# Interleaving the first block products of a second MLP with the last products of the first, on one Trainium2 core

## The chip, the cores and the metric

The kernel runs on one core of one Trainium2 chip. The metric is device time in microseconds, the median of several executions. A core has five engines with queues of their own: TensorE (PE, the matrix engine, whose weight loads are listed apart as PEld), VectorE (DVE), ScalarE (ACT), GpSimd (POOL) and SyncE (SP), which here only issues transfers. They wait for each other through semaphores; each works its own queue strictly in order.

## What is computed

Three stages on 2304 tokens, all in fp32 (cut to what matters):

```python
attn = softmax(mask(q @ k.T / sqrt(D))) @ v          # 4 x 8 heads, window 32, half of them dilated by 4
x  = attn laid out as (2304, 512)
xn = x / rms(x) * rms_g
u  = silu(xn @ w_gate) * (xn @ w_val)                # 1536 hidden
x  = u @ w_out                                       # (2304, 512)
h  = x @ w_in                                        # (2304, 1024)
e  = exp(h - max(h)); solu = h * e / sum(e)
ln = (solu - mean) / sqrt(var + 1e-6) * g_ln
out = ln @ w_out2                                    # (2304, 512)
```

## The kernel before, in words

**Products.** Every fp32 operand is split into a rounded high part and a rest, and a product is three matmuls: high by high, high by low, low by high (`mm3`, lines 849 to 851; 1110 to 1112; 1182 to 1184). One matmul has 512 columns.

**The first MLP** (`mlp`, 853) goes over the tokens in seven stretches; the last five of 512 tokens (the very last part, p = 4, has 512). For each of 12 blocks f of the hidden size: `g` (12 matmuls, gate), `vp` (12, value), then on ACT and DVE tanh (L880), two products (L886, L890) and the split into `uh` (L286, L295), and two blocks later `out` (12 matmuls into four accumulators y0 to y3). After the last block the accumulators are copied to `yo` (L286/L290) and stored to memory as `yT`.

**The second MLP** goes over pairs of tiles of 128 tokens, r = 0 to 8, two tiles each. One pair:

- `p_load` (1052) reads the pair's activations `y` back from `yT` with three transfers (L1056, L1058).
- `p_sums` (L1064) makes four sums of blocks, on POOL or DVE; `p_high` and `p_low` (L286, L295) split them into `yh`, first three blocks (128x768), then four (128x1024).
- Seven block products `p1` to `p7` of six matmuls each (`p_product`, L1110 to L1112): a Strassen-Winograd scheme, into accumulators `ha` to `hd`. p1, p6 and p7 add up in `ha`, and after each of them `ha` is copied out (s1, u2, u3: L286 or L290) before the next may write. p5 and p3 share `hb`. Four sums on DVE (`p_sum`, L1118; named c11, c12, c21, c22 below) put the rows of h together: c22 needs u3 and p5, c21 p4, c12 p3, c11 p2.
- For each of the two tiles (row 1, then row 0): exp (ACT, L1128), solu (DVE, L1135), square (ACT, L1142), centre (DVE, L1147) and a root on POOL (L1151, L1152).

One tile then takes eight transposes `t` (L1163), the split into `lt` (L286 on ACT, then L295 on DVE: "lt low"), 24 matmuls `o` (L1182 to L1184) in two halves of 12, an evacuation `ob` and a store (L1200).

**Order.** A planner (`Plan.order`, 165) gives every step an engine and a place from estimated costs, due times and needs; the instructions are then issued in that order, and each engine works its queue in order. For TensorE the order of the second MLP is written out by hand (the list `line`, 1299): each step is put behind the one ahead of it.

```python
line = [("out", last, NF1 - 1, 1)] + h(0, "p1", "p5", "p6", "p2", "p7", "p4") + h(1, "p1") + h(0, "p3") + \
    h(1, "p2", "p5", "p6", "p7", "p4", "p3") + t(0)
```

So no product of a pair is issued ahead of the first MLP's last `out`. The room for odd pairs' `y` and `yh` (pool `hp`) is opened by `switch` (1207), which needs all steps of the first MLP; only pair 0 (and 2, once 0 is done) has room earlier, where the attention's was.

Of the kernel before, what the change touches and what calls it, by code (L numbers as in the profile page):

```python
# [240 lines left out]
def tile_attention_glu_solu(ctx: ExitStack, tc: tile.TileContext, qk_d, v_d, w1_d, win2_d, wout2_d,  # L241
# [68 lines left out]

    def prepare(stage, f, cuts, srcs, scales, dues, needs=(), lead=((1, 0), "joined", 0)):

# [4 lines left out]
        def raw(c):  # L317
            if ("raw", key, c) not in T:
                T["raw", key, c] = wp.tile([P, len(c), 512, 2], I32, tag=f"w{f}_{c[0]}", name=f"raw{f}_{c[0]}")
            return T["raw", key, c]  # L320
# [34 lines left out]
        def halves(c):  # L355

            def emit(e):
                T["th", key, c] = wp.tile([P, len(c), 2, 512], F32R, tag=f"w{f}_{c[0]}", name=f"w{f}_{c[0]}")
                put(e, T["th", key, c][:, :, 0], wf_(c))
            return emit  # L360

        def lows(c):
            def emit(e):
                th = T["th", key, c]
                less(e, th[:, :, 1], wf_(c), th[:, :, 0])
                for i in c:
                    (w1 if stage == 1 else w2)[f, i] = th[:, i - c[0]]
            return emit
# [699 lines left out]
    def p_high(r, h, e):  # L1068
        if r not in pairs:
            pairs[r] = pool["y", r % 2].tile([P, 2, 7, 2, P], F32R, tag=f"yh{r % 2}", name="yh")  # L1070
        c = SETS[h]
        put(e, pairs[r][:, 0, c], y2[r][:, 1 + c.start:1 + c.stop])

    def p_low(r, h, e):
        c = SETS[h]
        less(e, pairs[r][:, 1, c], y2[r][:, 1 + c.start:1 + c.stop], pairs[r][:, 0, c])

# [26 lines left out]
    def p_product(r, a, b, bank, more):  # L1104
        o, yh = p_bank(r, bank), pairs[r]
        for j in range(2):
            x = LEFT[a]
            w = w_in[b, j]
            first, last_ = j == 0 and not more, j == 1
            nc.tensor.matmul(o, yh[:, 0, x, j], w[:, 0], start=first, stop=False, skip_group_check=True)  # L1110
            nc.tensor.matmul(o, yh[:, 0, x, j], w[:, 1], start=False, stop=False, skip_group_check=True)
            nc.tensor.matmul(o, yh[:, 1, x, j], w[:, 0], start=False, stop=last_, skip_group_check=True)  # L1112

# [60 lines left out]
    def p_products(i, ks, a=0, n=DM):  # L1174
# [5 lines left out]
        for k in ks:  # L1180
            w = w2[5 + k // 3, k % 3][:, :, a:a + n]
# [21 lines left out]
    def second_stage(stage_1, last):  # L1203
# [3 lines left out]
        def switch(e):  # L1207
            p1.close()
            pool["hp"] = pool["y", 1] = ctx.enter_context(tc.tile_pool(name="hp", bufs=1))

        def opened(e):
            pa.close()
            pool["y", 0] = ctx.enter_context(tc.tile_pool(name="yp", bufs=1, side="right"))
            pool["sp2"] = ctx.enter_context(tc.tile_pool(name="sp2", bufs=2, side="right"))
# [4 lines left out]
        def pair_steps(r):  # L1219
            due = base + 22 * (r - 2)  # L1220
            ys, yh, hw, ew = ((x + str(r % 2), (x, r)) for x in ("ys", "yh", "hw", "ew"))
            p = max(x for x in range(len(PARTS)) if start[x] <= r * TP)
            add(("load", r), {"s": 1.6}, lambda e: p_load(r), [("opened",) if r % 2 == 0 else ("switch",)] +
                [("store", p, k) for k in range(KD)], takes=[ys], due=due - 40)
            add(("sums", r), {"p": 2.9, "d": 1.4}, lambda e: p_sums(r, e), [("load", r)], uses=[ys[1]], due=due - 20)
            for h, (a, d) in enumerate(((0.85, 0.95), (1.1, 1.25))):
                add(("yhigh", r, h), {"a": a}, lambda e, h=h: p_high(r, h, e), [("load", r)] + ([("sums", r), ("yhigh", r, 0)] if h else []),
                    takes=[yh] if h == 0 else [], uses=[ys[1], yh[1]], due=due - 20)
                add(("ylow", r, h), {"d": d}, lambda e, h=h: p_low(r, h, e), [("yhigh", r, h)], uses=[ys[1], yh[1]], due=due - 20)
            banks = {x: ("h" + x, r) for x in "abcd"}  # L1230
            tags = dict(a="g", b="vp", c="a", d="a")

# [4 lines left out]
            def kept(x, after_, tile_, tags_):  # L1237
                add((x, r), {"a": 0.6, "d": 0.62}, lambda e: put(e, p_row(r, x), p_bank(r, "a")), [(after_, r)],
                    takes=tags_, uses=[banks["a"], tile_[1]], due=due - 60)

            def total(x, row, col, kept_, bank, n, before):
                add((x, r), {"d": 0.75}, lambda e: p_sum(r, row, col, kept_, bank, n), before + [(kept_, r)],
                    uses=[banks[bank], hw[1], ew[1]], due=due - 50)

# [13 lines left out]
            total("c12", 0, 1, "u2", "b", 1, [("p3", r), ("c11", r)])  # L1258
            for row in (1, 0):
                k = (r, row)  # L1260
                ends = [("c21", r)] if row else [("c12", r)]
                add(("neg", *k), {"d": 0.16}, lambda e, row=row: p_neg(r, row), ends, due=due - 10)
                add(("exp", *k), {"a": 1.3}, lambda e, row=row: p_exp(r, row), [("neg", *k)], uses=[hw[1], ew[1]], due=due)
                add(("solu", *k), {"d": 1.85}, lambda e, row=row: p_solu(r, row), [("exp", *k)], uses=[hw[1], ew[1]], due=due)
# [4 lines left out]
        def tile_steps(i):  # L1269
            r, row = divmod(i, 2)  # L1270
            due = base + 22 * r + 11 * row
            lt = ("lt", ("lt", i))
            for q in range(2):
# [4 lines left out]
                add(("lt", i, q, 1), {"d": 0.7}, lambda e, q=q: p_lt(i, q, 1, e), [("lt", i, q, 0)], uses=[tp[1], lt[1]], due=due - 60)  # L1278
            for a, n in ([(0, DM)] if i < NT2 - 1 else [(0, DM // 2), (DM // 2, DM // 2)]):
                o = (f"y{2 + (i + (a > 0)) % 2}", ("o", i, a))  # L1280
# [25 lines left out]
        line += [("o", NT2 - 1, a, q) for a in (0, DM // 2) for q in range(2)]  # L1306
        for x, y in zip(line, line[1:]):
# [29 lines left out]
    for j in range(2):  # L1337
        operands(j, done)
    for f in range(5, 8):
        us = range(3 * (f - 5), min(3 * (f - 5) + 3, NF2))  # L1340
        prepare(2, f, [(i,) for i in range(len(us))] if f < SINGLE else [tuple(range(len(us)))],
                [wout2_d[u] for u in us], [gln[:, u:u + 1] for u in us], [5070 + u for u in us], done(f), (("in", 0), "joined", "b11"))

    second_stage([x for x in plan.steps if x[0] not in ("evac", "store")], last)
# [92 lines left out]
```

## Time and profile before

| | |
|---|---|
| Time, median of 3 runs | 752.02 us (751.43 to 752.91) |
| The profiled execution | 749.95 us, span 748.2 us |
| PE busy | 734.1 us, 98% of the span |
| DVE, ACT, POOL busy | 59%, 43%, 17% |
| Granted clock of TensorE, mean | 0.995 |
| First MLP's last matmul to first `o` matmul | 537.3 to 567.9 us |

A busy PE is not one at its peak: matmuls overlap, so the distance between the starts of two matmuls that follow each other is the measure, and where it is longer than usual something was waited for or the clock was low. The timeline gives starts; the list of waits says which engine ended a wait; the windows give the granted clock of a stretch, where 1.00 is 2.4 GHz and 0.5 is 1.2 GHz.

### The profile page before, as it was taken

What the parts mean: (1) busy time and instruction counts of PE and PEld (TensorE: products, weight loads), DVE (VectorE), ACT (ScalarE), POOL (GpSimd) and SP (SyncE); (2) the same over time, 40 slices, a digit from 0 to 9 for tenths busy, and PEclk for the clock granted to TensorE, in tenths of its full rate; (3) what the DMA queues carried; (4) which work ended last, traced back from release to release, by engine and by line L of the source; (5) the groups of instructions that cost most, each with busy time, mean ns of one, the idle gap of its engine ahead of it and who ended that gap; (6) DMA issues with size and microseconds to landing.
All of it is one profiled execution on the core that took longest, in us unless ns stands there. A gap on an engine that the chain in (4) does not pass through costs nothing.

```text
span 748.2 us, 11769 instructions
## 1 busy us (share of the span) xinstructions
PE 734.1 (98%) x4637; PEld 613.0 (82%) x4637; DVE 439.3 (59%) x868; ACT 322.4 (43%) x734; POOL 130.7 (17%) x156
## 2 busy tenths in 40 slices
PE   8899999999999999999999999999989999999997
PEld 6788888899988888888887888888858888888886
DVE  4879996455433354434454438978278677655552
ACT  2876645355323233223334224534255555434340
POOL 0320322222300022300121204310023211001110
PEclk9999999999999999999999999999999999999999
DMA  8997003142121121041212036231111210101001
GB/s 330 405 404 275 26 11 111 69 150 88 39 88 37 39 75 51 1 157 37 82 55 74 1 94 228 72 113 56 60 54 54 66 52 29 47 25 28 30 29 42
DMA packets 34247, 68.91 MB, mean 92 GB/s; under 512 B 3344, under 2 KB 13584, under 8 KB 34192
## 3 DMA queue, kind: packets, MB, share of 16 engines
q1 hardware_dynamic: 34192, 68.16, 26.0%
q8 instruction: 36, 0.59, 0.3%
q14 instruction: 19, 0.16, 0.1%
HBM read 58.71 MB, written 9.44 MB: 91 GB/s over the span
## 4 chain that ended last, share of the span: by engine, by line
PE 94%; DMA 3%; DVE 1%; ACT 1%; SPq 0%; issue 0%; DVEq 0%
PE y L849 7%; PE g L849 7%; PE vp L849 7%; PE g L850 7%; PE g L851 7%; PE y L851 7%; PE y L850 7%; PE vp L851 7%; PE vp L850 7%; PE o L1183 4%; PE o L1184 4%; PE o L1182 4%; PE pv L631 2%; PE tp L1163 2%; PE sp L585 2%; PE ha L1112 2%
## 5 line engine op out<-in xcount | busy, mean ns | idle before, releaser
L849 PE MATMUL y<-uh,w 128*128 128x512 f32 (+1 forms) x244 | 91.6, 376 | 0.0
L851 PE MATMUL y<-uh,w 128*128 128x512 f32 (+1 forms) x244 | 89.2, 366 | 0.0
L850 PE MATMUL y<-uh,w 128*128 128x512 f32 (+1 forms) x244 | 89.1, 365 | 0.0
L886 DVE SCALAR_TENSOR_TENSOR u<-u,g 128x512 f32<-128x512 f32 (+1 forms) x61 | 38.1, 624 | 79.0 <-ACT u L880 78.6
L880 ACT ACTIVATE u<-g 128x512 f32<-128x512 f32 (+1 forms) x61 | 33.4, 547 | 118.4 <-PE g L851 118.4
L849 PE MATMUL vp<-xh,w 128*128 128x512 f32 (+1 forms) x196 | 77.9, 397 | 0.0
L849 PE MATMUL g<-xh,w 128*128 128x512 f32 (+1 forms) x196 | 77.6, 396 | 0.0
L850 PE MATMUL g<-xl,w 128*128 128x512 f32 (+1 forms) x196 | 75.9, 387 | 0.0
L851 PE MATMUL g<-xh,w 128*128 128x512 f32 (+1 forms) x196 | 75.9, 387 | 0.0
L851 PE MATMUL vp<-xh,w 128*128 128x512 f32 (+1 forms) x196 | 75.7, 386 | 0.0
L850 PE MATMUL vp<-xl,w 128*128 128x512 f32 (+1 forms) x196 | 75.5, 385 | 0.0
L890 DVE SCALAR_TENSOR_TENSOR u<-u,vp 128x512 f32<-128x512 f32 (+1 forms) x61 | 38.1, 625 | 49.9 <-PE vp L851 49.4
L286 ACT CAST uh<-u 128x512 fp32r<-128x512 f32 (+1 forms) x61 | 34.8, 570 | 74.0 <-DVE u L890 73.6
L1182 PE MATMUL o<-w,lt 128*128 128x512 f32 (+1 forms) x152 | 58.9, 388 | 0.0
L1184 PE MATMUL o<-w,lt 128*128 128x512 f32 (+1 forms) x152 | 57.6, 379 | 0.0
L1183 PE MATMUL o<-w,lt 128*128 128x512 f32 (+1 forms) x152 | 57.5, 379 | 0.0
L731 POOL TENSOR_TENSOR sq<-x 128x256 f32<-128x256 f32 x28 | 18.6, 666 | 211.6 <-DVE x L290 179.5
L295 DVE TENSOR_TENSOR uh<-u,uh 128x512 fp32r<-128x512 f32 (+1 forms) x61 | 43.8, 717 | 15.1 <-ACT uh L286 14.5
L849 PEld LDWEIGHTS y<-uh,w 128*128 128x128 f32 x244 | 46.0, 188 | 8.1
L851 PEld LDWEIGHTS y<-uh,w 128*128 128x128 f32 x244 | 46.0, 188 | 7.5
L850 PEld LDWEIGHTS y<-uh,w 128*128 128x128 f32 x244 | 46.1, 189 | 7.0
L598 ACT ACTIVATE s<-s,nm 128x64 f32<-128x64 f32 x120 | 40.2, 338 | 22.7 <-DVE nm L593 22.7
(165 smaller groups left out, 1580.5 us busy)
## 6 DMA issues: line engine op xcount, KB each, us to landing
raw<-w SPq DMA_DIRECT2D x36, 512.0 KB, 10.2
vt<-v SPq DMA_DIRECT2D x30, 256.0 KB, 2.7
qk<-qk SPq DMA_DIRECT2D x14, 400.0 KB, 3.5
yT<-yo SPq DMA_DIRECT2D x16, 256.0 KB, 2.5
raw<-win SPq DMA_DIRECT2D x8, 512.0 KB, 6.2
raw<-wout SPq DMA_DIRECT2D x8, 512.0 KB, 3.6
out<-ob SPq DMA_DIRECT2D x16, 256.0 KB, 2.0
qk<-qk SPq DMA_DIRECT2D x6, 448.0 KB, 4.2
```

Source lines behind the costliest of these rows:

```text
L286: nc.scalar.copy(dst, src) if scale is None else nc.scalar.mul(dst, src, scale)
L295: ENG[e].tensor_tensor(dst, a, b, ALU.subtract)
L598: nc.scalar.activation(T[s_][:, i], T[s_][:, i], AF.Exp, bias=st["nm"][:, i:i + 1], accum_out=sm[:, i:i + 1])
L849: nc.tensor.matmul(acc, wh, xh, start=first, stop=False)
L850: nc.tensor.matmul(acc, wh, xl, start=False, stop=False)
L851: nc.tensor.matmul(acc, wl, xh, start=False, stop=last)
L880: return lambda e: nc.scalar.activation(new(up, ("u", v, f), [P, 512])[:, 0:n], T["g", v, f], AF.Tanh, scale=0.5)
L886: return lambda e: nc.vector.scalar_tensor_tensor(out=u_of(f), in0=u_of(f), scalar=1.0, in1=T["g", v, f], op0=ALU.add, op1=ALU.mult)
L890: return lambda e: nc.vector.scalar_tensor_tensor(out=u_of(f), in0=u_of(f), scalar=0.5, in1=T["vp", v, f], op0=ALU.mult, op1=ALU.mult)
L1182: nc.tensor.matmul(o, lt[:, 0, k], w[:, 0], start=(k == 0), stop=False)
L1183: nc.tensor.matmul(o, lt[:, 0, k], w[:, 1], start=False, stop=False)
L1184: nc.tensor.matmul(o, lt[:, 1, k], w[:, 0], start=False, stop=(k == NF2 - 1))
```

## The change

The products of pair 0 are put between the products of the first MLP's last four blocks; pair 1's activations are loaded once the last but two `out` is issued, into the room of weight block 9, and its split parts go into room beside weight block 7 and into a tile of their own; pair 0's four accumulators use the two banks of tag `a` that the attention had; its c12 is summed ahead of its c11. In every pair the second tile goes ahead of the first through `t` and `o`. The weights of the last product move between blocks (one from block 7 to block 2). Pieces of the diff:

```diff
     def p_load(r):
-        y = pool["y", r % 2].tile([P, 8, 2, P], F32, tag=f"y{r % 2}", name="y")
+        if r == 0:
+            y = pool["yp"].tile([P, 8, 2, P], F32, tag="yl", name="y")
+        elif r == 1:
+            y = wp.tile([P, 8, 2, P], F32, tag="w9_0", name="y")
+        else:
+            y = pool["hp"].tile([P, 8, 2, P], F32, tag=f"y{r % 2}", name="y")
...
         if r not in pairs:
-            pairs[r] = pool["y", r % 2].tile([P, 2, 7, 2, P], F32R, tag=f"yh{r % 2}", name="yh")
+            if r % 2 == 0:
+                t = pool["yp"].tile([P, 2, 7, 2, P], F32R, tag="yh", name="yh")
+                pairs[r] = t[:, 0], t[:, 1]
+            else:
+                t = T["th", (2, 7), (0,)][:, 1:3].rearrange("p i h n -> p (i h n)")[:, 0:7 * TP]
+                pairs[r] = (t.rearrange("p (x j q) -> p x j q", x=7, j=2),
+                            pool["yp"].tile([P, 8, 2, P], F32R, tag="yl", name="yl")[:, 0:7])
...
+    SEQ = [i ^ 1 for i in range(NT2)]
+    OUT_AT = [(2, 2)] + [(f, i) for f in (5, 6) for i in range(3)] + [(7, 0)]
...
-            add(("load", r), {"s": 1.6}, lambda e: p_load(r), [("opened",) if r % 2 == 0 else ("switch",)] +
-                [("store", p, k) for k in range(KD)], takes=[ys], due=due - 40)
+            add(("load", r), {"s": 1.6}, lambda e: p_load(r), [("opened",) if r < 2 else ("switch",)] +
+                ([("out", last, 9, 1)] if r == 1 else []) + [("store", p, k) for k in range(KD)], takes=[ys],
+                due=due - 90 if r else 4900)
...
-            tags = dict(a="g", b="vp", c="a", d="a")
+            tags = dict(a="g", b="vp", c="a", d="a") if r else dict(a="a", b="a", c="a", d="a")
...
-            due = base + 22 * r + 11 * row
+            due = base + 22 * r + 11 * (1 - row)
...
-        line = [("out", last, NF1 - 1, 1)] + h(0, "p1", "p5", "p6", "p2", "p7", "p4") + h(1, "p1") + h(0, "p3") + \
-            h(1, "p2", "p5", "p6", "p7", "p4", "p3") + t(0)
+        def m(x, f):
+            return [(x, last, NF1 + f, i) for i in range(2)]
+
+        line = m("out", -4) + h(0, "p1") + m("g", -2) + h(0, "p5") + m("vp", -2) + h(0, "p6") + m("out", -3) + m("g", -1) + \
+            h(0, "p7") + m("vp", -1) + h(0, "p3") + m("out", -2) + h(0, "p2", "p4") + m("out", -1) + \
+            h(1, "p1", "p5", "p6", "p2", "p7") + t(SEQ[0]) + h(1, "p4", "p3")
         for q in range(NP):
-            a, b, r = 2 * q, 2 * q + 1, q + 2
-            line += h(r, "p1", "p5", "p6") + [("o", a, 0, 0)] + t(b) + [("o", a, 0, 1)] + h(r, "p2", "p7", "p4")
+            (a, b), r = SEQ[2 * q:2 * q + 2], q + 2
+            line += h(r, "p1", "p5", "p6") * (q > 0) + [("o", a, 0, 0)] + t(b) + [("o", a, 0, 1)] + \
+                h(r, "p1", "p5", "p6") * (q == 0) + h(r, "p2", "p7", "p4")
             if q < NP - 1:
-                line += [("o", b, 0, 0)] + h(r, "p3") + t(b + 1) + [("o", b, 0, 1)]
+                line += [("o", b, 0, 0)] + h(r, "p3") + t(SEQ[2 * q + 2]) + [("o", b, 0, 1)]
```

In the changed kernel the lines from 1056 on have moved: a product of a pair is at L1125 to L1127, a sum at L1133, the transposes at L1180, `o` at L1199 to L1201.

On TensorE, in the first MLP's last stretch, the change has this behind the fourth last `out` (y3 its last accumulator; win are the second MLP's weights, yh pair 0's split activations):

```order
L851 MATMUL y3_4572<-uh_5030,w8_0_1157 128x512
L1125 MATMUL ha_5109<-win_4633,yh_4577 128x512
L1126 MATMUL ha_5109<-win_4633,yh_4577 128x512
L1127 MATMUL ha_5109<-win_4633,yh_4577 128x512
L1125 MATMUL ha_5109<-win_4740,yh_4577 128x512
L1126 MATMUL ha_5109<-win_4740,yh_4577 128x512
```

This is p1 of pair 0. p5, p6, p7, p3, p2 and p4 follow in the same way between the `g`, `vp` and `out` that come after, where before all of them stood behind the last `out`.

On the SP queue, at the end of the first MLP, the loads of the pairs (y from yT, three transfers a pair) and the stores of the last results (yT from yo) stand so in the change:

```order
L324 DMA raw_0_5051<-wout 128x1024
L1061 DMA y<-yT_91 128x4x128
L1063 DMA y<-yT_91 128x2x128 x2
L957 DMA yT_95<-yo 128x512 x2
L1061 DMA y<-yT_92 128x4x128
```

Before, pair 1's load (from yT_91) stood behind all four of these stores. Now it stands ahead of them, and waits for the last matmul that reads weight block 9.

On VectorE, behind pair 0's centring (e) come pair 1's sums (h from hc, hb, hd, and hb again: c11, c22, c21, c12) and the first tile's lt low:

```order
L1162 TENSOR_SCALAR e<-e,st 128x1024 x2
L1133 ISA h,st<-h,hc 128x512
L1133 ISA st 128x1
L1133 ISA h,st<-e,hb 128x512
L1133 ISA st 128x1
L1133 ISA h,st<-e,hd,st 128x512
L1133 ISA st 128x1
L1133 ISA h,st<-h,hb,st 128x512
L1133 ISA st 128x1
L295 TENSOR_TENSOR lt<-tp,lt 128x512 x2
```

All four sums of pair 1 stand ahead of the first lt low. On TensorE the first `o` matmuls stand right behind p3 of pair 1, the product that the fourth of these sums reads; before, the eight transposes of a tile and three products of pair 2 stood between.

## Rows read from the trace of the kernel before

**Rows 1.** The page, part 1: busy us (share of the span) x instructions of each engine

```profile
PE 734.1 (98%) x4637; PEld 613.0 (82%) x4637; DVE 439.3 (59%) x868; ACT 322.4 (43%) x734; POOL 130.7 (17%) x156
```

**Rows 2.** TensorE's waits, whole span: us in total, times, longest us

```profile
PE ha L1112 <- DVE st L1133: 2.4, 1, 2.4
...
PE ha L1110 <- ACT h L286: 0.7, 1, 0.7
PE ha L1110 <- ACT yh L286: 0.3, 1, 0.3
```

**Rows 3.** Timeline of TensorE, 537 to 568 us: start, length (us), line, tiles, [idle <-releaser]

```profile
537.31 0.39 PE L1110 MATMUL ha<-win,yh 128*128 128x512 f32 x1
...
545.25 0.39 PE L1112 MATMUL hd<-win,yh 128*128 128x512 f32 x1
545.97 0.50 PE L1110 MATMUL ha<-win,yh 128*128 128x512 f32 x1 [0.33 <-ACT yh L286]
546.30 0.40 PE L1111 MATMUL ha<-win,yh 128*128 128x512 f32 x1
549.14 0.65 PE L1112 MATMUL ha<-win,yh 128*128 128x512 f32 x1 [2.45 <-DVE st L1133]
...
552.89 0.39 PE L1112 MATMUL hb<-win,yh 128*128 128x512 f32 x1
...
557.00 0.39 PE L1112 MATMUL ha<-win,yh 128*128 128x512 f32 x1
558.06 0.50 PE L1110 MATMUL ha<-win,yh 128*128 128x512 f32 x1 [0.68 <-ACT h L286]
...
562.80 1.09 PE L1163 MATMUL tp<-ident,e 128*128 128x128 f32 x8
563.65 0.47 PE L1110 MATMUL ha<-win,yh 128*128 128x512 f32 x1
...
567.86 0.39 PE L1182 MATMUL o<-w,lt 128*128 128x512 f32 x1
```

**Rows 4.** Busy us by stretch: length, PE, PEld, DVE, ACT, POOL, granted clock, DMA share, GB/s

```profile
34.00:45.00 11.00, 8.62 (x73) 8.10 (x73) 7.45 (x17) 7.95 (x16) 2.57 (x2) 1.00 1.03 409
545.60:549.10 3.50, 0.77 (x3) 0.30 (x2) 3.29 (x11) 2.40 (x4) 0.00 (x0) 1.00 0.01 2
549.10:553.00 3.90, 3.85 (x10) 3.05 (x11) 2.79 (x6) 1.92 (x4) 0.08 (x1) 0.56 0.00 0
```

**Rows 5.** Timeline of ScalarE, 545 to 564 us (columns as in rows 3)

```profile
545.08 0.83 ACT L286 CAST yh<-y 128x768 fp32r<-128x768 f32 x1 [0.18 <-DMA y<-yT]
...
557.42 0.58 ACT L286 COPY h<-ha 128x512 f32<-128x512 f32 x1 [0.57 <-PE ha L1112]
...
562.84 1.15 ACT L1128 ACTIVATE e<-h,st 128x1024 f32<-128x1024 f32 x1 [2.54 <-DVE st L1124]
```

**Rows 6.** Timeline of VectorE, 548 to 574 us

```profile
548.14 0.95 DVE L295 TENSOR_TENSOR yh<-y,yh 128x768 fp32r<-128x768 f32 x1
...
553.33 0.75 DVE L1118 CUSTOM_DVE_ANT_0 h<-h,hb,st 128x512 f32<-128x512 f32 x1 [1.33 <-PE hb L1112]
...
564.92 1.28 DVE L295 TENSOR_TENSOR lt<-tp,lt 128x512 fp32r<-128x512 f32 x2
...
566.49 1.28 DVE L1135 SCALAR_TENSOR_TENSOR e<-e,st,h 128x1024 f32<-128x1024 f32 x1
...
573.46 0.76 DVE L1147 TENSOR_SCALAR e<-e,st 128x1024 f32<-128x1024 f32 x1 [0.34 <-ACT sq L1142]
```

**Rows 7.** Timeline of GpSimd, 556 us

```profile
556.83 3.95 POOL L1064 TENSOR_TENSOR y<-y 128x256 f32<-128x256 f32 x4 [3.08 <-DMA y<-yT]
```

**Rows 8.** Timeline of the SP queue, 540 us

```profile
540.75 0.54 SPq L1056 DMA_DIRECT2D y<-yT  x1
```

**Rows 9.** Timeline of the SP queue, the end of the span

```profile
744.65 1.11 SPq L1200 DMA_DIRECT2D out<-ob  x2
```

**Rows 10.** Line L1200, the output stores: from issue to landing

```profile
DMA to landing us min/median/max: 1.9/2.0/2.6
```

More of the change, by code (lines that the diff above doesn't have):

```diff
@@ L309, in tile_attention_glu_solu, with prepare @@
     w1, w2 = {}, {}
-    def prepare(stage, f, cuts, srcs, scales, dues, needs=(), lead=((1, 0), "joined", 0)):
+    def prepare(stage, f, cuts, srcs, scales, dues, needs=(), lead=((1, 0), "joined", 0), at_=0, spare=0):
         key = (stage, f)
@@ L318, in raw @@
             if ("raw", key, c) not in T:
-                T["raw", key, c] = wp.tile([P, len(c), 512, 2], I32, tag=f"w{f}_{c[0]}", name=f"raw{f}_{c[0]}")
+                T["raw", key, c] = wp.tile([P, len(c), 512, 2], I32, tag=f"w{f}_{at_ + c[0]}", name=f"raw{f}_{c[0]}")
             return T["raw", key, c]
@@ L357, in emit @@
             def emit(e):
-                T["th", key, c] = wp.tile([P, len(c), 2, 512], F32R, tag=f"w{f}_{c[0]}", name=f"w{f}_{c[0]}")
-                put(e, T["th", key, c][:, :, 0], wf_(c))
+                T["th", key, c] = wp.tile([P, len(c) + spare, 2, 512], F32R, tag=f"w{f}_{at_ + c[0]}", name=f"w{f}_{c[0]}")
+                put(e, T["th", key, c][:, 0:len(c), 0], wf_(c))
             return emit
@@ L364, in emit @@
                 th = T["th", key, c]
-                less(e, th[:, :, 1], wf_(c), th[:, :, 0])
+                less(e, th[:, 0:len(c), 1], wf_(c), th[:, 0:len(c), 0])
                 for i in c:
-                    (w1 if stage == 1 else w2)[f, i] = th[:, i - c[0]]
+                    (w1 if stage == 1 else w2)[f, at_ + i] = th[:, i - c[0]]
             return emit
@@ L1069, in p_high @@
         if r not in pairs:
-            pairs[r] = pool["y", r % 2].tile([P, 2, 7, 2, P], F32R, tag=f"yh{r % 2}", name="yh")
+            if r % 2 == 0:
[5 more added lines that the diff above has]
+                            pool["yp"].tile([P, 8, 2, P], F32R, tag="yl", name="yl")[:, 0:7])
         c = SETS[h]
-        put(e, pairs[r][:, 0, c], y2[r][:, 1 + c.start:1 + c.stop])
+        put(e, pairs[r][0][:, c], y2[r][:, 1 + c.start:1 + c.stop])
     def p_low(r, h, e):
         c = SETS[h]
-        less(e, pairs[r][:, 1, c], y2[r][:, 1 + c.start:1 + c.stop], pairs[r][:, 0, c])
+        less(e, pairs[r][1][:, c], y2[r][:, 1 + c.start:1 + c.stop], pairs[r][0][:, c])
     LEFT = {"a11": 0, "a12": 1, "a22": 2, "s1": 3, "s2": 4, "s3": 5, "s4": 6}
@@ L1087, in p_row @@
     def p_row(r, x):
+        if x == "u3" and r == 0:
+            if (r, x) not in keep:
+                keep[r, x] = pool["yp"].tile([P, 512], F32, tag="u3", name="u3")
+            return keep[r, x]
         if x in ("s1", "u2") or x[0] == "h":
@@ L1109, in p_product @@
             first, last_ = j == 0 and not more, j == 1
-            nc.tensor.matmul(o, yh[:, 0, x, j], w[:, 0], start=first, stop=False, skip_group_check=True)
-            nc.tensor.matmul(o, yh[:, 0, x, j], w[:, 1], start=False, stop=False, skip_group_check=True)
-            nc.tensor.matmul(o, yh[:, 1, x, j], w[:, 0], start=False, stop=last_, skip_group_check=True)
+            nc.tensor.matmul(o, yh[0][:, x, j], w[:, 0], start=first, stop=False, skip_group_check=True)
+            nc.tensor.matmul(o, yh[0][:, x, j], w[:, 1], start=False, stop=False, skip_group_check=True)
+            nc.tensor.matmul(o, yh[1][:, x, j], w[:, 0], start=False, stop=last_, skip_group_check=True)
     def p_sum(r, row, col, kept, bank, n):
@@ L1208, in switch @@
             p1.close()
-            pool["hp"] = pool["y", 1] = ctx.enter_context(tc.tile_pool(name="hp", bufs=1))
+            pool["hp"] = ctx.enter_context(tc.tile_pool(name="hp", bufs=1))
         def opened(e):
             pa.close()
-            pool["y", 0] = ctx.enter_context(tc.tile_pool(name="yp", bufs=1, side="right"))
+            pool["yp"] = ctx.enter_context(tc.tile_pool(name="yp", bufs=1, side="right"))
             pool["sp2"] = ctx.enter_context(tc.tile_pool(name="sp2", bufs=2, side="right"))
@@ L1222, in pair_steps @@
             p = max(x for x in range(len(PARTS)) if start[x] <= r * TP)
-            add(("load", r), {"s": 1.6}, lambda e: p_load(r), [("opened",) if r % 2 == 0 else ("switch",)] +
-                [("store", p, k) for k in range(KD)], takes=[ys], due=due - 40)
-            add(("sums", r), {"p": 2.9, "d": 1.4}, lambda e: p_sums(r, e), [("load", r)], uses=[ys[1]], due=due - 20)
+            if r < 2:
+                ys = (("yh1", hw[0])[r], ys[1])
+            add(("load", r), {"s": 1.6}, lambda e: p_load(r), [("opened",) if r < 2 else ("switch",)] +
+                ([("out", last, 9, 1)] if r == 1 else []) + [("store", p, k) for k in range(KD)], takes=[ys],
+                due=due - 90 if r else 4900)
+            add(("sums", r), {"p": 2.9, "d": 1.4}, lambda e: p_sums(r, e), [("load", r)], uses=[ys[1]], due=due - 55 if r else 4900)
             for h, (a, d) in enumerate(((0.85, 0.95), (1.1, 1.25))):
-                add(("yhigh", r, h), {"a": a}, lambda e, h=h: p_high(r, h, e), [("load", r)] + ([("sums", r), ("yhigh", r, 0)] if h else []),
-                    takes=[yh] if h == 0 else [], uses=[ys[1], yh[1]], due=due - 20)
-                add(("ylow", r, h), {"d": d}, lambda e, h=h: p_low(r, h, e), [("yhigh", r, h)], uses=[ys[1], yh[1]], due=due - 20)
+                add(("yhigh", r, h), {"a": a}, lambda e, h=h: p_high(r, h, e), [("load", r)] + ([("sums", r), ("yhigh", r, 0)] + ([("uhigh", last, NF1 - 1)] if r == 1 else []) if h else [((2, 7), "halves", 0)] * (r % 2)),
+                    takes=[yh] if h == 0 else [], uses=[ys[1], yh[1]], due=due - 55 if r else 4900)
+                add(("ylow", r, h), {"d": d}, lambda e, h=h: p_low(r, h, e), [("yhigh", r, h)] + ([("ulow", last, NF1 - 1)] if (r, h) == (1, 1) else []), uses=[ys[1], yh[1]], due=due - 55 if r else 4900)
             banks = {x: ("h" + x, r) for x in "abcd"}
-            tags = dict(a="g", b="vp", c="a", d="a")
+            tags = dict(a="g", b="vp", c="a", d="a") if r else dict(a="a", b="a", c="a", d="a")
             def product(x, a, b, bank, more, before):
@@ L1238, in kept @@
                 add((x, r), {"a": 0.6, "d": 0.62}, lambda e: put(e, p_row(r, x), p_bank(r, "a")), [(after_, r)],
-                    takes=tags_, uses=[banks["a"], tile_[1]], due=due - 60)
+                    takes=tags_, uses=[banks["a"], tile_[1]], due=due - 60 if r else 4900)
             def total(x, row, col, kept_, bank, n, before):
                 add((x, r), {"d": 0.75}, lambda e: p_sum(r, row, col, kept_, bank, n), before + [(kept_, r)],
-                    uses=[banks[bank], hw[1], ew[1]], due=due - 50)
+                    uses=[banks[bank], hw[1], ew[1]], due=due - 50 if r else 4900)
             product("p1", "a11", "b11", "a", False, [])
@@ L1250, in pair_steps @@
             product("p2", "a12", "b21", "c", False, [])
-            total("c11", 0, 0, "s1", "c", 0, [("p2", r)])
+            total("c11", 0, 0, "s1", "c", int(r == 0), [("p2", r)] + [("c12", 0)] * (r == 0))
             product("p7", "s3", "t3", "a", True, [("u2", r)])
-            kept("u3", "p7", ew, [ew])
+            kept("u3", "p7", ew, [ew] if r else [])
             total("c22", 1, 1, "u3", "b", 0, [("p5", r)])
@@ L1257, in pair_steps @@
             product("p3", "s4", "b22", "b", True, [("c22", r)])
-            total("c12", 0, 1, "u2", "b", 1, [("p3", r), ("c11", r)])
+            total("c12", 0, 1, "u2", "b", int(r > 0), [("p3", r)] + [("c11", r)] * (r > 0))
             for row in (1, 0):
+                due = (due if r else 4950) + 1 + (row == 0)
                 k = (r, row)
-                ends = [("c21", r)] if row else [("c12", r)]
+                ends = [("c21", r)] if row else [("c12" if r else "c11", r)]
                 add(("neg", *k), {"d": 0.16}, lambda e, row=row: p_neg(r, row), ends, due=due - 10)
-                add(("exp", *k), {"a": 1.3}, lambda e, row=row: p_exp(r, row), [("neg", *k)], uses=[hw[1], ew[1]], due=due)
+                add(("exp", *k), {"a": 1.3}, lambda e, row=row: p_exp(r, row), [("neg", *k)] + ([("exp", 0, 1)] if k == (0, 0) else []),
+                    takes=[ew] if k == (0, 1) else [], uses=[hw[1], ew[1]], due=due)
                 add(("solu", *k), {"d": 1.85}, lambda e, row=row: p_solu(r, row), [("exp", *k)], uses=[hw[1], ew[1]], due=due)
@@ L1278, in tile_steps @@
                 add(("lt", i, q, 1), {"d": 0.7}, lambda e, q=q: p_lt(i, q, 1, e), [("lt", i, q, 0)], uses=[tp[1], lt[1]], due=due - 60)
-            for a, n in ([(0, DM)] if i < NT2 - 1 else [(0, DM // 2), (DM // 2, DM // 2)]):
+            for a, n in ([(0, DM)] if i != SEQ[-1] else [(0, DM // 2), (DM // 2, DM // 2)]):
                 o = (f"y{2 + (i + (a > 0)) % 2}", ("o", i, a))
@@ L1338, in tile_attention_glu_solu @@
         operands(j, done)
[L1339 to L1342, printed above, removed]
+    for f, us in ((2, (0,)), (5, (1, 2, 3)), (6, (4, 5, 6)), (7, (7,))):
+        prepare(2, f, [(i,) for i in range(len(us))], [wout2_d[u] for u in us], [gln[:, u:u + 1] for u in us],
+                [5070 + u for u in us], done(f), (("in", 0), "joined", "b11"), 2 if f == 2 else 0, 2 if f == 7 else 0)
     second_stage([x for x in plan.steps if x[0] not in ("evac", "store")], last)
```

4 lines of the change are left out of this document (2 added, 2 removed).

## The prediction

> **What bounds the kernel now.** I read the busy times first: TensorE is busy for 98% of the span [rows 1], so time can be gained only where it waits, runs at the low clock, or after its last matmul. Next, the list of TensorE's waits: the longest of the second half, 2.4 us, stands in front of `ha`, and two more of 0.7 and 0.3 us as well [rows 2]. The timeline then shows where they lie [rows 3]. From the first `ha` matmul at 537.31 to a matmul of `hd` at 545.25 there are 35 steps (from start to start) in 7.94 us, 0.227 us a step; this is the pace of unhindered matmuls of 512 columns. From 537.31 to the first `o` matmul at 567.86, 30.55 us, TensorE issues 102 such matmuls (14 products of pairs 0 and 1, three of pair 2, six matmuls each) and one set of transposes, 0.85 us long (562.80 to 563.65). 102 x 0.227 + 0.85 = 24.0 us. So 6.55 us are lost here. After this stretch a pair repeats at full pace, and the list of waits holds nothing for it.
>
> **What the lost time is made of** [rows 3].
> a) 545.25 to 549.14: three steps take 3.89 us in place of 0.68, so 3.21 lost. Pair 1's activations are late: their load is issued at 540.75 [rows 8], behind the whole first MLP, and is ready for ScalarE's cast at 545.08 [rows 5], 4.3 us later; sums and the low part follow, the latter until 549.09 [rows 6].
> b) 549.14 to 552.89: nine steps take 3.75 us in place of 2.04, so 1.71 lost. The granted clock of 549.10 to 553.00 is 0.56, that is for most of it the lower of the two levels (1.2 GHz in place of 2.4), after a stretch in which TensorE was busy for 0.77 of 3.50 us [rows 4].
> c) 557.00 to 558.06: one step of 1.06, so 0.83 lost; p7 of pair 1 stands right behind p6 and waits until `ha` is copied out.
> d) The remaining 0.80 are small: longer first steps after each wait, a short wait in front of p3, and the edges of the transposes.
>
> **What the change does to each.**
> Pair 0's seven products move in between the first MLP's matmuls. The matmuls stay the same in number, so this by itself gives nothing. It gives cover: once the last `out` is issued, pair 1's operands have long been there. Their load now waits for the third last `out` only. Behind that come g, p7, vp, p3, out, p2, p4 and out: 72 matmuls, 16.3 us. The path is 4.3 us to the cast, four sums on GpSimd 3.95 [rows 7], the cast of the four-block part (4/3 of 0.83, 1.1) and its low part (4/3 of 0.95, 1.3): 10.7 us. It fits with 5 us to spare, so a) goes, and with it b). c) goes because p2 now stands between p6 and p7 of pair 1: 1.36 us of matmuls over a copy of 0.58 [rows 5]. Of d) I take 0.5. Gained: 3.21 + 1.71 + 0.83 + 0.5 = 6.25 us; the bounds are 5.75 (nothing of d) and 6.55.
>
> The work that pair 0 hands to other engines must be hidden in the first MLP:
> - s1 (p1 to p6): 30 matmuls, 6.8 us, over a copy of 0.58. u2 (p6 to p7): 24 matmuls, 5.4 us. Both hidden.
> - u3 and c22 (p7 to p3): the 12 matmuls of vp, 2.72 us, over 0.2 (the end of the last matmul) + a copy of about 0.7 + 0.75 for the sum [rows 6]: 1.7. Hidden, 1.0 to spare.
> - c12 (p3 to p4, which writes the same bank): 18 matmuls, 4.1 us, over 0.75 and the low parts in the queue ahead of it, below 3 together. Hidden.
> - The chain from c21 to the first transposes of pair 0 is the tightest. TensorE has out and five products of pair 1 in between: 42 matmuls, 9.5 us. ScalarE: the sum ends at 0.9, exp 1.15 [rows 5], then a copy of an accumulator, the other row's exp and two more copies before the first square. Counted up with 0.6 for a copy and 1.15 for a square, it is done by 6.6; VectorE's centring of 0.76 [rows 6] stands behind the copy u2, which ends at 7.6. So 8.4 against 9.5. Hidden, 1.1 to spare.
> If one of these covers goes, its own excess is the price.
>
> The change adds one wait that nothing covers. The first `o` products stand right behind p3 of pair 1, and their third matmul needs lt low. On VectorE lt low stands behind c12 of pair 1, which reads what p3 writes. Counted from the start of p3's last matmul: it ends at 0.39 [rows 3], c12 takes 0.75 and the first of the two lt low half of 1.28 [rows 6], with small gaps 1.9 us. TensorE would issue the third `o` matmul at 3 x 0.227 = 0.68. A wait of 1.2 us, 1.3 with the longer step behind it. From below it can hardly be under 1.0, since the order is fixed; from above it is 1.3 plus the low clock, of which more below. Behind the waiting matmul the rest of TensorE's queue waits; nothing else there is late.
>
> In the repeating part (pairs 2 to 8) each tile has the same work. The row whose sums, exp and solu come first is now also transposed first, which gives slack where there was enough. I take 0.
>
> The end: the last tile was tile 17, whose rows fall into two stretches of the output; now it is tile 16, in one. The last store is one transfer in place of two, and the two take 1.11 us to issue [rows 9]. Half of this, 0.55 us, goes. Bounds: 0 if the larger transfer lands later by as much (landing takes 1.9 to 2.6 us [rows 10]), 0.65 at most.
>
> **The sum.** -6.25 + 1.3 - 0.55 = -5.5 us. Against the profiled execution's own 749.95 us that is 744.45. The median of the runs shown, 752.02, stands 2.07 above that execution; the time I forecast is such a median, 746.5 us.
>
> **Rivals.**
> B, the new wait lowers the clock. For: at 546.7 a wait of 2.45 us was followed by nine steps at half pace, 1.71 us. Against: the stretch from 34.00 to 45.00 holds an idle time of 2.4 us (11.00 less the busy share) at a granted clock of 1.00 [rows 4], and the wait in c) did no harm either. Price: 1.7, so 748.2 us. 10%. The Trainium skill, page "TensorE: Matmul & The Clock Gate", section "HAM oscillation — how this bites in real kernels", tells of a kernel in which a wait between bursts of matmuls sent each next burst back to the cold clock; by it the time would be this 748.2. The trace agrees with it for the wait at 546.7 us and not for the earlier one.
>
> C, pair 0's chain to the first transposes is late. For: 1.1 us is little, and ScalarE's copy of the last accumulator waits until a buffer is stored (a store lands after 2 us [rows 10]). Each further copy or store in the way costs 0.6 to 2 us, less the 1.1. Price about 1.2: 747.7 us. 10%.
>
> D, the new wait does not show because VectorE is ahead. Against: the order of its queue. 745.2 us. 4%.
>
> E, slower. In the repeating part the copies s1 and u2 come behind an exp of 1.15 us on ScalarE. A copy has 1.36 + 0.23 - 0.39 - 0.58 - 0.08, about 0.54 us to spare under p5 or p2. Were it held up for a whole exp, TensorE would wait 0.6 us twice in each of seven pairs: +8.5, 755.0 us. It turns the gain into a loss from 0.4 us of wait for each copy on. For: the new order of tiles moves the exp's, and one now stands right ahead of a copy. Against: before, 18 such copies caused a single wait of 0.7 [rows 2]. 6%; in half of it the waits eat the gain only.
>
> **How the numbers follow.** The forecast as worked out has 70%. What a measurement of this kernel can tell from no change is about 0.2%, 1.5 us. A, B, C and D are all faster by more, and of E none is: 94% faster, 3% within 0.2%, 3% slower. The forecast's own bounds: downwards 0.3 (all of d), 0.3 (a new wait of 1.0) and 0.1 (end), so 745.8; upwards 0.5 (nothing of d) and 0.55 (nothing at the end), so 747.55. For 8 in 10 the range takes in B above (748.2) and D below (745.2), and half a microsecond on each side for the scatter of the median (751.43 to 752.91 before): 744.7 to 748.7.
>
> **What will show it.** Right: the first MLP's last four blocks with pair 0 between them run at 0.227 us a step with no wait; pair 1's products follow without one at full clock; TensorE waits once, for about 1.2 us, at the third `o` matmul (L1201), ended by VectorE's lt low; the steps behind it stay at 0.227; the last store is a single one. Wrong: waits of TensorE inside the last `g`, `vp` or `out`, or in front of the first transposes (C); steps of 0.43 behind the new wait (B); repeated waits at p6 or p7 (E). The whole account is wrong if the stretch runs without waits and the time is still not shorter by 4 us or more.

## The result, and the profile after

Faster, by 0.9%. The median is 744.86 us (744.28 to 746.55, four runs) against 751.72 us (750.32 to 752.91, four runs) of the kernel before: a ratio of 0.9913, 95% interval [0.9889, 0.9937]. Forecast were 746.5 us and a range of 744.7 to 748.7. The profiled execution took 744.79 us, its span 743.0 us at a mean granted clock of 0.997.

The busy times of the kernel after, from the page (part 1; engine, busy us, share, instructions):

```profile
PE 730.7 (98%) x4637; PEld 611.8 (82%) x4637; DVE 436.1 (59%) x868; ACT 323.7 (44%) x737; POOL 134.0 (18%) x158
```

Beside [rows 1] hardly anything moves: TensorE has the same 4637 matmuls and the same 98%. That line alone tells nothing of the change. TensorE's waits in the whole span after do (waited for: us in total, times, longest us):

```profile
PE sp L453 <- DMA qkv<-qk: 3.7, 3, 2.5
PE g L304 <- DVE u L886: 2.3, 1, 2.3
PE rs L766 <- DMA raw<-w: 1.0, 1, 1.0
PE o L1201 <- DVE lt L295: 1.0, 1, 1.0
PE warm L304 <- POOL half L1375: 0.9, 1, 0.9
```

Against [rows 2] the three waits in front of `ha` are gone, and one at `o` (L1201) is new. The other four lie in the first 50 us, which no edit touches: up to 450 us each engine has the same work in the same order in all the kernels of this document.

These first 50 us scatter from execution to execution (more on that at the end), so the two traces are compared from a point that both pass in the same way: the start of the first `y` matmul of block 2 in the first MLP's last stretch. In the timeline of TensorE before (start, length in us, line, tiles) that point and the last matmul of all are:

```profile
466.59 0.39 PE L849 MATMUL y<-uh,w 128*128 128x512 f32 x1
...
743.82 0.28 PE L1184 MATMUL o<-w,lt 128*128 128x256 f32 x1
```

And the timeline of TensorE after, from that point over the place of the change to the last matmul:

```profile
467.64 0.39 PE L849 MATMUL y<-uh,w 128*128 128x512 f32 x1
...
538.36 0.39 PE L1125 MATMUL hb<-win,yh 128*128 128x512 f32 x1
...
547.65 0.39 PE L851 MATMUL y<-uh,w 128*128 128x512 f32 x1
547.88 0.39 PE L1125 MATMUL ha<-win,w 128*128 128x512 f32 x1
...
554.68 1.03 PE L1180 MATMUL tp<-ident,e 128*128 128x128 f32 x8
...
558.52 0.39 PE L1200 MATMUL o<-w,lt 128*128 128x512 f32 x1
559.90 0.50 PE L1201 MATMUL o<-w,lt 128*128 128x512 f32 x1 [1.00 <-DVE lt L295]
560.24 0.40 PE L1199 MATMUL o<-w,lt 128*128 128x512 f32 x1
...
739.63 0.28 PE L1201 MATMUL o<-w,lt 128*128 128x256 f32 x1
```

From the common point to the last matmul it was 743.82 - 466.59 = 277.23 us, and is 739.63 - 467.64 = 272.00 (rounded in the last digit): 5.23 less. From the last matmul to the end of the span it was 4.35 us (span 748.17), and is 3.37 (743.01): 0.98 less. Together 6.21. The execution after reached the common point 1.05 later, and so its span is 5.16 shorter.

The row at 547.88 is the heart of it: the first product of pair 1 starts one step of 0.23 us behind the last `out`. Before, at this place, [rows 3] showed two waits and nine steps at half pace. The windows of the kernel after (stretch, length, busy us of PE, PEld, DVE, ACT, POOL, granted clock, DMA share, GB/s):

```profile
519.30:547.90 28.60, 28.60 (x128) 23.67 (x127) 11.75 (x24) 6.33 (x10) 2.88 (x4) 1.00 0.07 21
547.90:558.50 10.60, 10.60 (x52) 8.88 (x51) 7.94 (x20) 8.14 (x15) 5.95 (x10) 1.00 0.62 196
558.50:560.00 1.50, 0.50 (x3) 0.10 (x1) 1.50 (x4) 0.81 (x2) 1.50 (x3) 1.00 0.01 5
560.00:566.00 6.00, 6.00 (x31) 5.05 (x32) 5.77 (x9) 2.39 (x4) 0.39 (x1) 1.00 0.29 81
```

TensorE is busy through the last blocks of the first MLP and pair 1's products (28.60 of 28.60, 10.60 of 10.60), stands still only in the third stretch, and has the full clock (1.00, 2.4 GHz) in all four, where [rows 4] had 0.56 for 3.9 us.

### The profile page after: what moved, and what is told of

Its sections match the earlier page's. It is cut to its first block, busy times and chain, and to the rows that moved or that the text cites. A ratio compares the mean times of both kernels' runs of the same rounds, so it can differ in the third digit from the quotient of the medians.

```text
span 743.0 us, 11770 instructions
## 1 busy us (share of the span) xinstructions
PE 730.7 (98%) x4637; PEld 611.8 (82%) x4637; DVE 436.1 (59%) x868; ACT 323.7 (44%) x737; POOL 134.0 (18%) x158
## 4 chain that ended last, share of the span: by engine, by line
PE 95%; DMA 3%; ACT 0%; DVE 0%; issue 0%; SPq 0%; DVEq 0%
PE y L849 7%; PE g L849 7%; PE vp L849 7%; PE g L851 7%; PE g L850 7%; PE y L851 7%; PE y L850 7%; PE vp L851 7%; PE vp L850 7%; PE o L1201 4%; PE o L1199 4%; PE o L1200 4%; PE pv L631 2%; PE tp L1180 2%; PE sp L585 2%; DMA qkv<-v 2%
## 5 line engine op out<-in xcount | busy, mean ns | idle before, releaser
L1199 PE MATMUL o<-w,lt 128*128 128x512 f32 (+1 forms) x152 | 58.9, 388 | 0.0
L1201 PE MATMUL o<-w,lt 128*128 128x512 f32 (+1 forms) x152 | 57.7, 380 | 1.0 <-DVE lt L295 1.0
L1200 PE MATMUL o<-w,lt 128*128 128x512 f32 (+1 forms) x152 | 57.5, 379 | 0.0
L295 DVE TENSOR_TENSOR uh<-u,uh 128x512 fp32r<-128x512 f32 (+1 forms) x61 | 45.5, 745 | 14.0 <-ACT uh L286 13.4
```

Source lines behind the costliest of these rows:

```text
L295: ENG[e].tensor_tensor(dst, a, b, ALU.subtract)
```

## The experiments

All are compared with the changed kernel by the same two distances. The starts are those of the timelines; all times in us.

| kernel | time | common point | last matmul | between | last matmul to end |
|---|---|---|---|---|---|
| before | 751.72 | 466.59 | 743.82 | 277.23 | 4.35 |
| after | 744.86 | 467.64 | 739.63 | 272.00 | 3.37 |
| lt low first | 742.82 | 469.71 | 740.45 | 270.74 | 3.37 |
| early load only | 747.49 | 467.95 | 742.24 | 274.28 | 3.36 |
| late load | 754.64 | 466.51 | 749.50 | 282.99 | 3.37 |
| last pair in old order | 744.17 | 466.05 | 738.05 | 272.01 | 4.35 |
| first tile first | 748.73 | 470.05 | 742.61 | 272.55 | 4.35 |
| longer wait | 749.86 | 468.16 | 744.69 | 276.53 | 3.37 |

The times of the first four are medians of several runs; the last four are one run each. They are from three sets of runs: the first two rows from one; the next four from a second, in which the kernel before had a median of 750.33 us (14 runs); the last two from a third, in which it had 751.68 us (one run). So times of different sets do not compare to the microsecond, and what the experiments show is read from their traces.

**1. The new wait alone: lt low ahead of c12.** In pair 1 the sum c12 now needs both lt low of the first tile, so VectorE takes them first.

```diff
-            total("c12", 0, 1, "u2", "b", int(r > 0), [("p3", r)] + [("c11", r)] * (r > 0))
+            total("c12", 0, 1, "u2", "b", int(r > 0), [("p3", r)] + [("c11", r)] * (r > 0) + [("lt", 1, q, 1) for q in range(2)] * (r == 1))
```

> Theory: the wait at the third `o` matmul (1.0 us of idle, 1.3 with the longer step behind it) comes from VectorE's order alone; with both lt low of the first tile ahead of c12 of pair 1 it vanishes and no other wait takes its place: about 1.2 us less than the changed kernel's 744.86, so 743.6 us. Rival: VectorE is short of time there, and the later c12 or centring moves a wait of the same size to p1, p5 or the next transposes of pair 2: the same time as the changed kernel, with a new row in TensorE's list of waits.

Measured: 742.82 us (742.65 to 745.62, five runs), 0.9894 [0.9876, 0.9912] of before. Its waits of TensorE are only those of the start:

```profile
PE sp L453 <- DMA qkv<-qk: 3.6, 3, 1.8
PE g L304 <- DVE u L886: 2.2, 1, 2.2
PE rs L766 <- DVE rd L761: 1.3, 2, 1.0
PE warm L304 <- POOL half L1375: 0.9, 1, 0.9
```

VectorE at that place, in the kernel after and then in this one (timeline: start, length, line, tiles, [idle <-releaser]):

```profile
558.49 0.75 DVE L1133 CUSTOM_DVE_ANT_0 h<-h,hb,st 128x512 f32<-128x512 f32 x1 [0.61 <-PE hb L1127]
...
559.16 1.28 DVE L295 TENSOR_TENSOR lt<-tp,lt 128x512 fp32r<-128x512 f32 x2
```

```profile
559.88 1.28 DVE L295 TENSOR_TENSOR lt<-tp,lt 128x512 fp32r<-128x512 f32 x2
561.08 0.74 DVE L1133 CUSTOM_DVE_ANT_0 h<-h,hb,st 128x512 f32<-128x512 f32 x1
```

The distance to the last matmul is 270.74, that is 1.26 less than after, and 1.26 is what the wait costs there: the step from 558.52 to 559.90 is 1.38 long and the next 0.34, where 0.23 each is the pace. So the wait was the order of VectorE's queue and nothing else, all of it stood on the path, and the sum put off is missed by nobody. Its distance is the shortest of all. By medians it is 7.51 us below the kernel before of its own set, and the change was 6.86 below that of its set, but the intervals of the two ratios overlap; what shows the gain is the trace.

**2. The early load without the interleaving.** Pair 1's load stays early, in its new room. Pair 0's products stand behind the last `out` again, with the banks and the order of sums of before; the second tile still goes first. The piece of the edit that orders TensorE's queue:

```diff
-        line = m("out", -4) + h(0, "p1") + m("g", -2) + h(0, "p5") + m("vp", -2) + h(0, "p6") + m("out", -3) + m("g", -1) + \
-            h(0, "p7") + m("vp", -1) + h(0, "p3") + m("out", -2) + h(0, "p2", "p4") + m("out", -1) + \
-            h(1, "p1", "p5", "p6", "p2", "p7") + t(SEQ[0]) + h(1, "p4", "p3")
+        line = m("out", -1) + h(0, "p1", "p5", "p6", "p2", "p7", "p4") + h(1, "p1") + h(0, "p3") + \
+            h(1, "p2", "p5", "p6", "p7", "p4", "p3") + t(SEQ[0])
```

> All of the change except the interleaving: pair 0's products stand behind the last `out` as before, pair 1's load is still early. Theory: the early load is what pays. The wait of 2.45 us and the half clock behind it (3.2 + 1.7 us) do not come back; what comes back are small waits with no cover: c12 of pair 0 in front of p5 of pair 1 (1.4), the copy u2 (0.9), c22 in front of p3 of pair 1 (1.1). Minus the changed kernel's own 1.2 that is about 2.2 us above it: 747 us, granted clock 1.00 in the stretch. Rival 1: the interleaving pays and the load by itself moves nothing: 750 us or more, with a wait of over 2 us for pair 1's operands. Rival 2: the interleaving is not needed at all: within 0.5 us of the changed kernel.

Measured: 747.49 us (745.80 to 750.01, nine runs), 0.9954 [0.9941, 0.9968] of before; the distance is 274.28, that is 2.28 more than after and 2.95 less than before. TensorE's waits behind the start:

```profile
PE hb L1125 <- DVE st L1133: 2.0, 2, 1.6
...
PE ha L1125 <- ACT h L286: 0.7, 1, 0.7
```

The granted clock stays at 1.00 around them (columns as in the windows above):

```profile
550.00:556.00 6.00, 4.09 (x17) 2.74 (x15) 5.33 (x15) 4.19 (x7) 4.38 (x5) 1.00 0.00 0
```

So of the 5.23 us of the stretch 2.95 come with the early load and the order of tiles (pair 1's activations and, with that wait gone, the half clock), and the other 2.28 when the interleaving is added. Without the products of the first MLP in between, TensorE is again faster than the sums and copies between two products of the same bank: `hb` waits for a sum, and `ha` for a copy, the latter as in [rows 2].

**3. The interleaving with a late load.** Pair 1's load waits for the very last `out`, not the last but two.

```diff
-                ([("out", last, 9, 1)] if r == 1 else []) + [("store", p, k) for k in range(KD)], takes=[ys],
+                ([("out", last, 11, 1)] if r == 1 else []) + [("store", p, k) for k in range(KD)], takes=[ys],
```

> All of the change, but pair 1's load waits for the last `out` of the first MLP. Theory: interleaving without the early load is worse than nothing, since pair 0's products no longer cover the load: waits of about 6.1 us in front of p1 of pair 1 (4.3 to the cast, cast, low part) and 1.8 us in front of p5 or its third matmul (sums on GpSimd), the low clock behind them (1.7), a copy wait of 0.7; the wait at `o` may go. About 9 us above the changed kernel: 754 us. Rival: the interleaved products alone make the gain and the load is off the path: 745 us.

Measured: 754.64 us in one run; the distance is 282.99, 10.99 more than after and 5.76 more than before. TensorE's waits at this place:

```profile
PE ha L1125 <- ACT w L286: 5.4, 1, 5.4
...
PE ha L1125 <- ACT h L286: 1.7, 1, 1.7
PE ha L1127 <- DVE yl L295: 1.7, 1, 1.7
```

Its windows (columns as above) from the last `out` on:

```profile
546.50:552.30 5.80, 0.41 (x2) 0.00 (x0) 4.87 (x14) 5.27 (x10) 1.35 (x4) 0.76 0.73 221
552.30:555.30 3.00, 1.26 (x3) 0.54 (x3) 3.00 (x6) 1.88 (x2) 1.08 (x2) 0.50 0.93 288
555.30:561.50 6.20, 4.56 (x10) 3.10 (x10) 2.31 (x3) 1.48 (x2) 6.04 (x7) 0.65 0.24 78
561.50:564.00 2.50, 2.40 (x10) 1.99 (x11) 1.05 (x1) 0.64 (x2) 2.36 (x2) 1.00 0.01 4
```

The interleaving alone is worse than nothing: it uses up pair 0's products, which had covered pair 1's load before, and then nothing stands over the load. The waits together are 8.87 us, 7.87 more than after; the remaining 3.1 come from the low clock and the longer first steps behind the waits. That is more than was expected, and the windows say why: the granted clock fell in the wait of 5.39 and stayed low over the next wait, of 1.74, into the third stretch, some ten microseconds in all, in which 12 matmuls ran between the waits. The third wait, expected at 0.7 us, was 1.74 too: on ScalarE the copy of `ha` stood behind a cast of pair 2's activations.

**4. The last pair of tiles in the old order.** Everything else as in the change; the last pair goes first tile, second tile (with due times and accumulators turned to suit, not shown).

```diff
-    SEQ = [i ^ 1 for i in range(NT2)]
+    SEQ = [i ^ 1 for i in range(NT2 - 2)] + [NT2 - 2, NT2 - 1]
```

> The changed kernel with the last pair's tiles in the old order (its accumulators' banks turned to suit), so that the last store is two transfers again. Theory: from TensorE's last matmul to the end of the span 4.35 us as before in place of 3.37, nothing else changes: 1.0 us above the changed kernel, measured from a common point in the first MLP. Rival: the end got shorter by chance of the landing, and the two transfers end within 0.3 us of the one.

Measured: 744.17 us in one run. The distance to the last matmul is 272.01, as after; from there to the end it is 4.35, as before. So the end's 0.98 us is the order of the last pair alone. The time itself does not show the loss, since this execution came through its start 1.6 us sooner.

**5. First tile first in all pairs.**

```diff
-    SEQ = [i ^ 1 for i in range(NT2)]
+    SEQ = list(range(NT2))
...
-            due = base + 22 * r + 11 * (1 - row)
+            due = base + 22 * r + 11 * row
```

> The changed kernel with the first tile of every pair ahead of the second, as before. Theory (the prediction took 0 for the tile order in the repeating part): pairs 3 to 8 run without a wait either way. Where the stages meet it does matter: the first tile's exp, solu and square come behind the second tile's, so tile 2's centring is late and its transposes wait, up to 1.7 us; the wait at the third `o` matmul may go, since VectorE's order moves; and the end is 4.35 us again. From a common point in the first MLP to TensorE's last matmul 272.5 us (changed kernel 272.0), to the end 1.5 us more. Rival 1: the order of tiles is neutral, same wait at `o`, 272.0 us, and only the end costs 1.0. Rival 2: it is worth a wait in every pair: 3 us or more on the way to the last matmul.

Measured: 748.73 us in one run; the distance is 272.55, that is 0.55 more than after, and the end is 4.35. The wait at `o` is gone and another stands in front of the third set of transposes, pair 1's first:

```profile
PE tp L1180 <- DVE e L1162: 1.6, 1, 1.6
```

Behind 581.11 us, where this wait is, TensorE waits no more: the order of the tiles costs or gives nothing in the repeating part. It decides where the two stages meet, by which of two waits VectorE's queue makes, and at the end.

**6. The same wait, longer.** To see what the clock does behind a longer wait at the same matmul, lt low of the first tile also needs the low parts of pair 2's activations, some 3 us of VectorE.

```diff
-                add(("lt", i, q, 1), {"d": 0.7}, lambda e, q=q: p_lt(i, q, 1, e), [("lt", i, q, 0)], uses=[tp[1], lt[1]], due=due - 60)
+                add(("lt", i, q, 1), {"d": 0.7}, lambda e, q=q: p_lt(i, q, 1, e), [("lt", i, q, 0)] + [("ylow", 2, h) for h in range(2)] * (i == 1), uses=[tp[1], lt[1]], due=due - 60)
```

> The changed kernel with the first tile's lt low put behind pair 2's low parts on VectorE, so that the wait at the third `o` matmul grows from 1.0 to about 3.2 us. What it tells is the clock: the changed kernel's 1.0 us and 1.65 us in the run with the load alone left the granted clock at 1.00, 2.45 us in the kernel before lowered it for nine matmuls. Theory: a wait of about 3 us is followed by 0.5 for a stretch like that one, so that the price is 2.2 us of wait and 1.7 us of slow steps: 276 us from the common point to the last matmul (272.0). Rival: the clock stays at 1.00 and the price is the wait alone: 274.2 us.

Measured: 749.86 us in one run; the distance is 276.53, that is 4.53 more than after. TensorE's timeline there:

```profile
563.35 0.50 PE L1201 MATMUL o<-w,lt 128*128 128x512 f32 x1 [3.92 <-DVE lt L295]
...
564.17 0.63 PE L1201 MATMUL o<-w,lt 128*128 128x512 f32 x1
564.60 0.63 PE L1199 MATMUL o<-w,lt 128*128 128x512 f32 x1
...
568.13 0.48 PE L1199 MATMUL o<-w,lt 128*128 128x512 f32 x1
```

The wait is 2.92 longer than after, and behind it seven steps in a row are 0.43: the lower level, 1.2 GHz. The windows from 562 to 566 and from 566 to 570 us have a granted clock of 0.76 and 0.81. The other 1.6 us are this. So rival B was a real danger: at this matmul a wait of 3.92 was followed by the lower clock, and the change's own 1.00 was not.

## Why the prediction was right, and which term was off

**Gain a) to c), pair 1's wait, the half clock and the copy.** Right. None of them is left after. The cover for the load came out as worked out: the load was issued at 531.75 us, ScalarE's cast began 4.2 us later (forecast 4.3), and the last low part ended 10.7 us after the issue (forecast 10.7), 5.4 before pair 1's first product (forecast 5); p5, the first to read this part, reads it at 549.69. Rows of the SP queue, ScalarE, GpSimd and VectorE after, from their timelines:

```profile
531.75 0.56 SPq L1061 DMA_DIRECT2D y<-yT  x1
```

```profile
535.91 0.84 ACT L286 CAST w<-y 128x768 fp32r<-128x768 f32 x1 [0.77 <-DMA y<-yT]
...
539.80 1.05 ACT L286 CAST w<-y 128x1024 fp32r<-128x1024 f32 x1
```

```profile
536.10 2.96 POOL L1069 TENSOR_TENSOR y<-y 128x256 f32<-128x256 f32 x4 [18.02 <-DMA y<-yT]
```

```profile
536.56 0.69 DVE L1133 CUSTOM_DVE_ANT_0 h<-u,hb 128x512 f32<-128x512 f32 x1
...
541.24 1.22 DVE L295 TENSOR_TENSOR yl<-y,w 128x1024 fp32r<-128x1024 f32 x1
...
552.76 1.41 DVE L1162 TENSOR_SCALAR e<-e,st 128x1024 f32<-128x1024 f32 x2
```

That the 10.7 came out so exactly is partly luck: the four sums took 2.96 us and not the 3.95 of [rows 7], and the cast and the low part behind them then stood in their queues for about as long (the cast began at 539.80, 0.7 behind the last sum, the low part at 541.24, 0.4 behind the cast).

Experiment 3 is the proof from the other side: with the load late, the wait for pair 1's activations and the low clock are back, and larger.

**The covers of pair 0's copies and sums.** Right. c22 (VectorE's row at 536.56) is done at 537.25 and p3 starts at 538.36: 1.1 to spare, forecast 1.0. The first centring is done about 0.7 us behind 552.76, at 553.5, and the transposes start at 554.68: 1.2 to spare, forecast 1.1. Here the links fit as well as the total: VectorE's copy u2, which the centring stands behind, ended 7.7 us after the start of the last `out` (forecast 7.6). This settles rival C: the chain was not late.

**The small losses d).** I took 0.5 of 0.80; 0.74 went. Without the new wait the stretch would be 5.23 + 1.26 = 6.49 us shorter, against 5.75 for a) to c) and, with all of d), 6.55. The small losses were hardly items of their own: nearly all of them went with the waits.

**The new wait.** Right: at the third `o` matmul, ended by lt low; 1.00 idle by the list and 1.26 us on the path, forecast 1.3. Experiment 1 takes it away and gets just these 1.26. So rival D (it does not show) falls.

**Rival B, the clock.** It did not come: 1.00 in the window behind the wait. Where the two stages meet, waits of 1.00 (after, and again in experiment 4) and 1.65 (experiment 2) left the clock at its higher level, and those of 2.45 (before), 3.92 (experiment 6) and 5.39 (experiment 3) went with the lower one. What the Trainium skill tells on the page "TensorE: Matmul & The Clock Gate", section "HAM oscillation — how this bites in real kernels", that in one kernel a wait between bursts sent each next burst back to the cold clock, agrees with the last three; the others show that not every wait does it.

The length of the wait alone does not decide. Near 40 us all eight traces have the wait `g` (L304) of the lists. Behind it the clock stayed at 1.00 in five (2.38 us before, 2.29 after, 2.40, 2.23 and 2.24 in experiments 3, 4 and 6) and was at 0.50 soon after in three (2.16, 2.23 and 2.24 us in experiments 1, 2 and 5). Experiments 2 and 6 even have the same two waits there, 1.04 and 2.23 against 1.05 and 2.24 us, in front of the same matmuls. A window that begins 1.4 us behind the second wait, of experiment 2 and then of 6:

```profile
40.00:43.00 3.00, 3.00 (x17) 2.07 (x15) 0.91 (x2) 0.68 (x2) 1.27 (x1) 0.50 1.03 407
```

```profile
41.80:44.80 3.00, 3.00 (x28) 2.83 (x27) 0.94 (x2) 0.71 (x2) 1.28 (x1) 1.00 1.03 410
```

So a wait of over 2 us can go either way from one execution to the next; what decides stays open here, and for the waits of 1.00 and 1.65 there are two traces and one.

**Rival E, the repeating part.** None of its waits came; experiment 5 shows that there the order of the tiles is worth nothing, as taken.

**The end: the term that was mis-sized.** I took half of the 1.11 us that the two stores need to be issued, 0.55. It was 0.98. After, SyncE's timeline ends with a single row:

```profile
740.46 0.34 SPq L1217 DMA_DIRECT2D out<-ob  x1
```

In both kernels the first store is issued 0.83 us behind the last matmul. From there to the end of the span it was 748.17 - 744.65 = 3.52, and is 743.01 - 740.46 = 2.55. Of this difference 0.77 is the issue: the one store needs 0.34 us, not the half of 1.11 [rows 9]. The bound of 0.65 was therefore too tight. The rest, 0.2, comes behind the last issue, where I had let the larger store only lose.

**The total.** The sum was -5.5 and the traces show -6.21: 0.28 of the difference lies in the stretch (nearly all d), 0.43 at the end. The medians differ by 6.86; for the 0.65 beyond the traces no step of the change accounts; it is less than what the start scatters by. Another 0.30 is that the forecast was added to 752.02, and the kernel before now has 751.72. So the forecast lay 1.6 above the measured 744.86. This is below the worked-out bound of 745.8 and below rival D's 745.2; the range's low end, 744.7, held it only by the half microsecond allowed for scatter. Of the bounds on the side of a larger gain the end's was too near; that of d held.

## What to carry to other kernels

Where two stages meet and the second has to fetch what the first has stored, issue the fetch as soon as its room is free and put the second stage's first products between the first's last ones; do both, since here the fetch alone gave 2.95 of 5.23 us and the interleaving with a late fetch lost 5.76. Then look at each in-order queue at the seam: a step that nobody needs soon (c12) ahead of one that TensorE waits for (lt low) cost 1.26 us, and turning them round was one dependency more. End with a result that goes out in one piece.

## What the runs showed of the hardware

**The cost of a wait depends on the clock as well as on its length, and the length alone does not tell whether the clock falls.** The waits of 2.45 and 3.92 us cost about 1.7 and 1.6 more for the half clock behind them. In experiment 3, where a second wait of 1.74 followed while the clock was low, it was some 3.1. I had expected one price for each fall. And of eight waits of 2.16 to 2.40 us at one place three were followed by the half clock and five were not.

**The start of this kernel scatters more than most of these edits are worth.** No edit touches the first 60 us. Yet the eleventh `y` matmul of line 849 started at 66.52 us before, 67.36 after, and in the six experiments at 69.64, 67.88, 66.44, 65.97, 69.98 and 68.09: 4.0 us from the first to the last. In the same order the waits for the first loads (the row `sp` L453 of the lists) were 1.9, 3.7, 3.6, 2.5, 1.7, 2.1, 5.3 and 4.9 us in total. In the earliest (experiment 4) the clock did not fall there at all, nor in experiment 6, which was late with long waits; in experiment 1, late with shorter ones, it fell twice. That loads and clock set the start together is read from these eight and was not tried by itself. It is why the distances from a common point decide here, and not single times.
